# GFNet mixing and a tanh-shrink MLP on one core: other Fourier factors, on folded rows, each batch alone

## The chip, the cores and the metric

The kernel runs on one core of a Trainium2 chip. The core has five engines that run side by side, each through its own queue in order: PE (TensorE, matrix products), DVE (VectorE), ACT (ScalarE), POOL (GpSimd) and SP (SyncE, which here only issues DMAs). PE's weight loads are a row of their own in the profile (PEld). The metric is the device time of one execution in microseconds (us), the median of several runs.

## The reference, cut to what matters

```python
def _attn_ref(x, filt_r, filt_i):            # x: 8 x 3008 x 256, float32
    X = np.fft.rfft(x, axis=1)
    F = (filt_r + 1j * filt_i)[None, :, :]   # 1505 x 256
    y = np.fft.irfft(X * F, n=x.shape[1], axis=1)
    return y.astype(np.float32)

def _moe_ref(x, w_in, w_out):                # x: 24064 x 256
    h = x @ w_in                             # 256 x 2048, given in float64
    g = h - np.tanh(h)
    return (g @ w_out).astype(np.float32)    # 2048 x 256
```

Each batch's 3008 rows are transformed along the sequence, multiplied by a complex filter that all batches share, and transformed back. All 24064 rows then go through a two-layer network with the function h - tanh(h) between.

## The kernel before, in words

3008 is 64 x 47, so a row number is 47 q + r with q from 0 to 63 and r from 0 to 46. The Fourier transform is done in two factors, and its inverse in two more, so the attention has three stages:

- **first** (`first`, L344; `first0`, L890, for batch 0): 64-point transforms over q for two values of r at a time. One constant 128x128 matrix `wf1` holds two 64x64 blocks, so two batches (a pair) share one product of 512 columns. ACT copies the result (`a1`) and stores it in DRAM (`ct1`).
- **middle** (`middle`, L401): 32 slots, one for each conjugate pair of frequencies. A slot has its own 94x128 matrix `f2` (47-point transform and twiddle factors) and its own 112x96 way back `g`, which `load_slots` (L376) fetches four at a time. After the product `pz` (L436), ACT writes the swapped halves (`zs`, L449 and L450), DVE multiplies `pz` by the filter's real part (`uv`, L451), and POOL multiplies `zs` by the imaginary part and adds (L452, L453). `back` does the product `pe` (L417), ACT copies it (`e1`, L420) and stores it in DRAM (`ct2`).
- **last** (`last`, L506): for a group of four r, products of `e2` (read from `ct2`) with the 128x128 matrix `s2`; the result `ut` stands with features on partitions, as the network needs it.

Batches are taken in units: batch 0 alone, pairs (1,2), (3,4), (5,6), and batch 7 alone. In a unit of two batches, a group is four values of r by 128 rows, 512 tokens. There are 46 groups.

The network works on one group in four passes; pass U has a quarter of the hidden width. The two big products use seven block products instead of eight (`combine`, L529, makes the sums that this needs), with half of a group's tokens (256 columns) at a time. Three functions overlap: `up(U)` (L538) makes h for pass U, `shrink(U-1)` (L613) makes h - tanh(h) for the pass before in about the form h * (sq + K) * y with ACT and DVE (L632 and L639 are DVE's two operations of 1024 columns, two of each in a pass), and `down(U-2)` (L668) multiplies by the second weights. At the end of `shrink`, POOL's `combine` (L530 to L533) makes the four tiles `t` from h, and PE's products `o<-t` (L688) of the following pass read them. The results are turned by DVE (L738) and leave in many small stores on SP (L781).

The order on every engine is written out by hand. A pass calls `t(0)` to `t(4)`, five places in which one step of the next unit's transforms may be put: a batch that stands alone has 6 groups x 4 passes x 5 = 120 such positions. The list `steps` (L1101 to L1108) gives each step of `first` and `middle` its position; two of the places in every fourth pass belong to `last`. So while PE works through the network for one unit, the transforms of the next unit lie between its products, and their DVE, ACT and POOL parts lie in those engines' queues at the same places.

PSUM's eight banks are x, y, z and t, one each, and the four of `down`; the transforms' products use t and y in turn (`zd`, L1052). In `up`, the first product of a pass overwrites x, so it waits until DVE has read x (L602).

Before all passes there is a preparation: batch 0 goes through first and middle, the weights of the network, which come in float64, are turned to float32 by DVE's integer operations (`converted`, L195), and POOL makes their sums (L264 to L267). The filter is read by POOL's DMAs (L916). During the first unit, POOL also copies the filter into the layout that `middle` reads (`filters_d`, L1068).

After the passes, a small reduction (`bounded`) decides whether a general form of the network has to run on the data; it doesn't run here.

Of the kernel before, what the change touches and what calls it, by code (L numbers as in the profile page):

```python
# [9 lines left out]
F32 = mybir.dt.float32  # L10
# [7 lines left out]

BATCH, SEQ, DM = 8, 3008, 256
NQ, NR = 64, 47
NK = NQ // 2
R2 = 2 * NR

RP = 48
RP2 = 2 * RP
LO = (NR + 1) // 2
HI = NR - LO  # L30
IM = 64
DFF = 2048
NP = DFF // 256
BD = 2 * DM
CH = 4
XH = 2


UNITS = [(0,), (1, 2), (3, 4), (5, 6), (7,)]
HALF = (NR + 1) // 2  # L40

EARLY = 2


def steps_of(unit):
    return NR if len(unit) == 2 else HALF


def chunks_of(unit, size):
    n = steps_of(unit)  # L50
    return [(r, min(size, n - r)) for r in range(0, n, size)]


# [5 lines left out]


# [4 lines left out]


def _consts():
    wq = np.exp(-2j * np.pi * np.outer(np.arange(NQ), np.arange(NQ)) / NQ)
    wr = np.exp(-2j * np.pi * np.outer(np.arange(NR), np.arange(NR)) / NR)
    tw = np.exp(-2j * np.pi * np.outer(np.arange(NQ), np.arange(NR)) / SEQ)  # L70


    f1 = np.zeros((NQ, 64))
    f1[:, 0:31] = wq.real[:, 1:32]
    f1[:, 31] = wq.real[:, 0]
    f1[:, 32:63] = wq.imag[:, 1:32]
    f1[:, 63] = wq.real[:, 32]


    wf1 = np.zeros((2, 128, 64, 2))  # L80
    wf0 = np.zeros((64, 2, 2, 64))
    for b in range(2):
        wf0[:, b, b] = f1
        wf1[0, 64 * b:64 * b + 64, :, b] = f1
        wf1[1].reshape(128, 2, 64)[64 * b:64 * b + 64, b] = f1
    wf1 = wf1.reshape(2, 128, 128).transpose(1, 0, 2)

    perm = np.arange(NR)  # L90
    perm[LO:] = LO + NR - 1 - perm[LO:]
    f2 = np.zeros((NK, R2, R2))
    for a in range(31):
        wp = (wr * tw[a + 1][None, :])[perm, :]
        f2[a, 0::2] = np.concatenate([wp.real.T, wp.imag.T], axis=1)
        f2[a, 1::2] = np.concatenate([-wp.imag.T, wp.real.T], axis=1)
    f2[:, :, NR + LO:] *= -1.0
    w0, w32 = wr * tw[0][None, :], wr * tw[32][None, :]
    f2[31, 0::2, 0:LO] = w0.real.T[:, 0:LO]
    f2[31, 0::2, NR + 1:NR + LO] = w0.imag.T[:, 1:LO]  # L100
    f2[31, 1::2, LO:NR] = w32.real.T[:, 0:HI]
    f2[31, 1::2, NR + LO:R2] = w32.imag.T[:, 0:HI]
    f2[31, 1::2, NR] = w32.real.T[:, HI]


    f2w = np.zeros((NK, R2, 128))
    f2w[:, :, 0:NR], f2w[:, :, IM:IM + NR] = f2[:, :, :NR], f2[:, :, NR:]


    ctw = np.exp(2j * np.pi * np.outer(np.arange(33), np.arange(NR)) / SEQ)  # L110
    g = np.zeros((NK, IM + NR, R2))
    for a in range(31):
        t1 = (wr.conj() * ctw[a + 1][:, None]) / SEQ
        tr, ti = t1.real.T[perm, :], t1.imag.T[perm, :]
        g[a, :NR, :NR], g[a, :NR, NR:] = tr, ti
        g[a, IM:, :NR], g[a, IM:, NR:] = -ti, tr
    g[:, IM + LO:] *= -1.0
    t0 = (wr.conj() * ctw[0][:, None] / SEQ).T
    t32 = (wr.conj() * ctw[32][:, None] / SEQ).T
    g[31, 0, :NR] = t0.real[0]  # L120
    g[31, IM, NR:] = t32.real[HI]
    g[31, 1:LO, :NR], g[31, IM + 1:IM + LO, :NR] = 2 * t0.real[1:LO], -2 * t0.imag[1:LO]
    g[31, LO:NR, NR:], g[31, IM + LO:, NR:] = 2 * t32.real[0:HI], -2 * t32.imag[0:HI]


    w = np.exp(2j * np.pi * np.outer(np.arange(NQ), np.arange(33)) / NQ)
    s = np.zeros((64, NQ))
    s[0:62:2] = 2.0 * w.real[:, 1:32].T
    s[1:62:2] = -2.0 * w.imag[:, 1:32].T
    s[62] = w.real[:, 0]  # L130
    s[63] = w.real[:, 32]
    s2 = np.zeros((128, 128))
    for b in range(2):
        s2[64 * b:64 * b + 64, 64 * b:64 * b + 64] = s


    fg = np.zeros((IM + RP, NK, 128 + RP2))
    fg[:R2, :, :128] = f2w.transpose(1, 0, 2)
    fg[:IM + NR, :, 128:].reshape(IM + NR, NK, 2, RP)[..., :NR] = \
        g.transpose(1, 0, 2).reshape(IM + NR, NK, 2, NR)  # L140

    return [np.ascontiguousarray(v, dtype=np.float32)
            for v in (wf0.reshape(128, 128), wf1, fg.reshape(IM + RP, -1), s2, np.eye(128))]


@with_exitstack
def kernel(
# [11 lines left out]
    wf0_d, wf1_d, fg_d, s2_d, one_d = (  # L159
        nc.inline_tensor(v, name=n).ap()  # L160
        for v, n in zip(_consts(), ("wf0", "wf1", "fg", "s2", "one")))


    ct1 = [nc.dram_tensor(f"ct1_{p}", (RP, 64 * len(bs), DM), F32, kind="Internal")
           for p, bs in enumerate(UNITS)]
    ct2 = [nc.dram_tensor(f"ct2_{p}", (64 * len(bs), RP, DM), F32, kind="Internal")
           for p, bs in enumerate(UNITS)]

    filt_d = nc.dram_tensor("filt", (IM, 2, NK, DM), F32, kind="Internal")
# [6 lines left out]
    wf1 = cst.tile([128, 2, 128], F32, name="wf1_sb")  # L176
    s2 = cst.tile([128, 128], F32, name="s2_sb")
    near_b = cst.tile([128, 1], F32, name="near_b")
    exp_b = cst.tile([128, 1], F32, name="exp_b")
    groups = [(p, c) for p, bs in enumerate(UNITS) for c in range(len(chunks_of(bs, CH)))]  # L180
    count = cst.tile([1, 1], I32, name="count")

# [5 lines left out]


# [78 lines left out]

# [50 lines left out]
    def halves(p, r, n):  # L327

        return [(h, slice(64 * h, 64 * h + 64), r + HALF * h, min(n, NR - r - HALF * h))
                for h in range(2) if r + HALF * h < NR]  # L330

    def load_x(p, r, n):
        t = tr.tile([128, XH, DM], F32, tag="x", bufs=3, name="x_sb")
        b = UNITS[p][0]
        if len(UNITS[p]) == 2:
            nc.sync.dma_start(t[:, 0:n, :], dram(x.tensor, (b * SEQ + r) * DM,
                                                 [[NR * DM, 128], [1, n * DM]]))
        else:
            for _, rows, r_h, n_h in halves(p, r, n):
                nc.sync.dma_start(t[rows, 0:n_h, :], dram(x.tensor, (b * SEQ + r_h) * DM,  # L340
                                                          [[NR * DM, 64], [1, n_h * DM]]))
        return t

    def first(p, z):  # L344

        chunks = chunks_of(UNITS[p], XH)
        pair = len(UNITS[p]) == 2
        xs = {c: load_x(p, *chunks[c]) for c in range(2)}
        yield
        for c, (r, n) in enumerate(chunks):  # L350
            if c + 2 < len(chunks):
                xs[c + 2] = load_x(p, *chunks[c + 2])
            xt = xs.pop(c)
            pf = z("pf", [128, XH, DM])
            a1 = tr.tile([128, XH, DM], F32, tag="a1", bufs=2, name="a1")
            if pair:
                nc.tensor.matmul(pf[:, 0:n, :], wf1[:, 0], xt[:, 0:n, :], start=True, stop=True)  # L357
                ACT.copy(a1[:, 0:n, :], pf[:, 0:n, :])  # L358
                ACT.dma_start(
                    dram(ct1[p], r * 128 * DM, [[DM, 128], [128 * DM, n], [1, DM]]),  # L360
                    a1[:, 0:n, :])
            else:
                parts = halves(p, r, n)
# [852 lines left out]
```

## Time and profile before

| | |
|---|---|
| Median of 3 runs | 2796.31 us (2794.76 to 2798.26) |
| Profiled execution, span from first to last instruction | 2793.9 us |
| PE busy | 2718.0 us (97%), 12436 records |
| DVE busy | 1914.7 us (69%) |
| ACT busy | 1883.9 us (67%) |
| POOL busy | 1759.4 us (63%) |
| DMA | 217.66 MB, 78 GB/s over the span |
| First product of the passes | at 113.6 us of the span |

The span of the profiled execution leaves 2.4 us to the median of the runs. A float32 product of the kernel is two weight loads and two MATMUL records in the trace. PE's records overlap each other, so their lengths don't add up; what a product costs is read from when the next one starts. In the lists of groups, a row gives line, engine, operation, out<-in, shapes and count, then total busy us and mean ns of one, then the idle time of the engine before them and what ended it.

### The profile page before, as it was taken

What the parts mean: (1) busy time and instruction counts of PE and PEld (TensorE: products, weight loads), DVE (VectorE), ACT (ScalarE), POOL (GpSimd) and SP (SyncE); (2) the same over time, 40 slices, a digit from 0 to 9 for tenths busy, and PEclk for the clock granted to TensorE, in tenths of its full rate; (3) what the DMA queues carried; (4) which work ended last, traced back from release to release, by engine and by line L of the source; (5) the groups of instructions that cost most, each with busy time, mean ns of one, the idle gap of its engine ahead of it and who ended that gap; (6) DMA issues with size and microseconds to landing.
All of it is one profiled execution on the core that took longest, in us unless ns stands there. A gap on an engine that the chain in (4) does not pass through costs nothing.

```text
span 2793.9 us, 36447 instructions
## 1 busy us (share of the span) xinstructions
PE 2718.0 (97%) x12436; PEld 2272.7 (81%) x12436; DVE 1914.7 (69%) x2190; ACT 1883.9 (67%) x2785; POOL 1759.4 (63%) x1399
## 2 busy tenths in 40 slices
PE   5899999999999999999999999999999999999998
PEld 3577778888878888888888888888888888898887
DVE  5776666666776777665677776766676667677777
ACT  3466776666767777666677777666666666666665
POOL 6456887444776777544576777654476666555553
PEclk8999999999999999999999999999999999999999
DMA  9854443332332322223323233112223222101010
GB/s 267 222 170 116 107 124 76 89 84 72 81 82 72 73 69 59 64 78 89 83 69 75 71 80 84 38 43 66 59 66 78 65 57 58 31 19 26 16 22 18
DMA packets 322095, 217.66 MB, mean 78 GB/s; under 512 B 224718, under 2 KB 274746, under 8 KB 321596
## 3 DMA queue, kind: packets, MB, share of 16 engines
q1 hardware_dynamic: 265994, 156.69, 24.1%
q10 hardware_dynamic: 52562, 50.09, 5.8%
q0 software_dynamic: 3344, 8.46, 1.1%
q8 instruction: 100, 1.64, 0.2%
q14 instruction: 95, 0.78, 0.1%
HBM read 139.00 MB, written 79.17 MB: 78 GB/s over the span
## 4 chain that ended last, share of the span: by engine, by line
PE 83%; DVE 5%; ACT 4%; DMA 2%; issue 2%; POOL 1%; ACTq 0%; SPq 0%; DVEq 0%; POOLq 0%
PE o L688 35%; PE x L551 21%; PE z L551 10%; PE y L551 5%; PE pe L417 3%; PE pz L436 3%; PE pu L517 3%; PE pf L357 2%; DVE h L632 2%; ACT y L628 1%; DMA raw<-in_moe_w_out_dram 1%; DVE h L602 1%; ACT y L625 1%; DVE h L639 1%; ACT sq L636 0%
## 5 line engine op out<-in xcount | busy, mean ns | idle before, releaser
L632 DVE TENSOR_TENSOR h<-h,y 128x1024 f32<-128x1024 f32 (+2 forms) x384 | 576.9, 1502 | 306.2 <-ACT y L628 305.1
L688 PE MATMUL o<-t,wd 128*128 128x256 f32 (+2 forms) x3072 | 774.4, 375 | 0.0
L688 PEld LDWEIGHTS o<-t,wd 128*128 128x128 f32 x3072 | 579.4, 190 | 90.9 <-issue 22.0
L639 DVE SCALAR_TENSOR_TENSOR h<-sq,h 128x1024 f32<-128x1024 f32 (+2 forms) x384 | 557.4, 1451 | 117.2 <-ACT sq L636 109.2
L688 PE MATMUL o<-h,wd 128*128 128x256 f32 (+2 forms) x2304 | 582.3, 375 | 6.8 <-DVE h L639 6.8
L551 PE MATMUL x<-tu,wu 128*128 128x256 f32 (+2 forms) x2304 | 582.0, 375 | 2.2 <-ACT u L557 2.1
L530 POOL TENSOR_TENSOR t<-h 128x512 f32<-128x512 f32 (+2 forms) x190 | 238.5, 1256 | 542.6 <-DVE h L639 385.3
L551 PEld LDWEIGHTS x<-tu,wu 128*128 128x128 f32 x2304 | 430.3, 190 | 103.0 <-issue 41.6
L688 PEld LDWEIGHTS o<-h,wd 128*128 128x128 f32 x2304 | 430.5, 190 | 80.4 <-issue 15.8
L636 ACT ACTIVATE sq<-y,near_b 128x1024 f32<-128x1024 f32 (+2 forms) x384 | 435.1, 1133 | 6.7 <-ACT y L628 0.3
L625 ACT ACTIVATE y<-h 128x1024 f32<-128x1024 f32 (+2 forms) x384 | 397.4, 1035 | 15.2 <-ACT e L420 6.4
L628 ACT ACTIVATE y<-y 128x1024 f32<-128x1024 f32 (+2 forms) x384 | 399.9, 1042 | 6.6 <-ACT a L358 0.4
L557 ACT COPY s<-x 128x512 f32<-128x512 f32 (+2 forms) x192 | 110.7, 577 | 327.9 <-PE x L551 301.7
L533 POOL TENSOR_TENSOR t<-t,h 128x512 f32<-128x512 f32 (+2 forms) x190 | 318.1, 1674 | 0.0
L557 ACT COPY u<-x 128x512 f32<-128x512 f32 (+2 forms) x384 | 220.7, 575 | 138.2 <-PE x L551 119.3
L531 POOL TENSOR_TENSOR t<-h,t 128x512 f32<-128x512 f32 (+2 forms) x190 | 244.2, 1285 | 14.9
L532 POOL TENSOR_TENSOR t<-h 128x512 f32<-128x512 f32 (+2 forms) x190 | 243.4, 1281 | 0.0
L452 POOL TENSOR_TENSOR zs<-zs,ft 128x512 f32<-128x512 f32 x112 | 164.9, 1472 | 93.5 <-ACT zs L450 93.3
L453 POOL TENSOR_TENSOR uv<-uv,zs 128x512 f32<-128x512 f32 x112 | 207.7, 1855 | 9.1 <-DVE uv L451 0.5
L551 PE MATMUL x<-ut,wu 128*128 128x256 f32 (+2 forms) x768 | 198.6, 381 | 9.7 <-DVE h L602 8.3
L594 DVE TENSOR_TENSOR h<-z,u 128x512 f32<-128x512 f32 (+2 forms) x192 | 128.8, 671 | 112.8 <-ACT u L557 111.9
L551 PE MATMUL z<-tu,wu 128*128 128x256 f32 (+2 forms) x768 | 195.2, 377 | 0.0
(129 smaller groups left out, 3294.0 us busy)
## 6 DMA issues: line engine op xcount, KB each, us to landing
a<-ct SPq DMA_DIRECT2D x64, 384.0 KB, 4.1
ft<-filt SPq DMA_DIRECT2D x96, 256.0 KB, 4.6
out_dram<-ot SPq DMA_DIRECT2D x1392, 16.0 KB, 1.5
ct<-e ACTq DMA_DIRECT2D x112, 192.0 KB, 2.2
ct<-a ACTq DMA_DIRECT2D x81, 256.0 KB, 2.9
x_sb<-in_x_dram SPq DMA_DIRECT2D x69, 256.0 KB, 2.9
e<-ct SPq DMA_DIRECT2D x33, 512.0 KB, 4.2
fg<-fg SPq DMA_DIRECT2D x40, 392.0 KB, 4.0
```

The costliest lines, as they stand in the source:

```text
L530: by.tensor_sub(t[0], b[0][1], b[0][0])
L531: by.tensor_sub(t[1], b[1][1], t[0])
L532: by.tensor_sub(t[2], b[1][1], b[0][1])
L533: by.tensor_sub(t[3], t[1], b[1][0])
L551: nc.tensor.matmul(bank[:, k], wu[:, q - 1, (2 * u + k) * 128:(2 * u + k + 1) * 128], rhs[q - 1], start=(first and k == 0), stop=True, ski ...
L557: ACT.copy(t, X)
L625: ACT.activation(y[k], ht[k], AF.Arctan, scale=S)
L628: ACT.activation(y[k], y[k], AF.Square, accum_out=y_sums[:, 2 * U + k // 2:2 * U + k // 2 + 1])
L632: V.tensor_mul(ht[k], ht[k], y[k])
L636: ACT.activation(sq[k], y[k], AF.Square, bias=near_b, scale=A)
L639: V.scalar_tensor_tensor(out=ht[k], in0=sq[k], scalar=K, in1=ht[k], op0=ALU.add, op1=ALU.mult)
L688: nc.tensor.matmul(product(q), wd[:, q - 1, (2 * u + k) * 128: (2 * u + k + 1) * 128], rhs[q - 1][:, k], start=(u == 0 and k == 0 and q == ...
```

## The change

The two factors are kept (64 and 47), but the work is cut another way.

- r and 47 - r are folded into one: only r = 0 to 23 are taken (`NH` = 24), with row r of the input on 64 partitions and row 47 - r on the other 64. Row 0 has no partner; it is loaded twice and its second matrix half is zero.
- The twiddle factors go into the first and the last matrices. So each r has its own dense 128x128 matrix, `f` for `first` (products of 256 columns, two to a step) and `gt` for `last`; both are loaded from DRAM next to the data, where `wf1` and `s2` lay in SBUF throughout.
- What is left between are real cosine and sine matrices of 24x24, the same for all frequencies. Five frequencies stand side by side on 120 partitions (`SG` = 5, `SLOTS`: six groups of five and one of two, seven slot groups for the 32 slots), and one constant tile `mats` holds their matrices; `fg` and `load_slots` are gone.
- In a slot group (`forth`, `filtered`, `back`; 8 products of 256 columns), the data are four blocks of 256. PE makes two and two products `pa`; ACT copies two blocks into `xy`; DVE adds and subtracts (L333, L334). POOL then multiplies the four blocks by the filter's real part (L343, 1024 columns) and by the imaginary part (L346, 1024 columns), and does four operations of 512 columns (L348, L349, L351, L352). PE goes back with four products `pe`, ACT copies them in two pieces (L365) and stores them. For batch 0, in the preparation, L343 and L346 are DVE's.
- Every batch stands alone: there are no pairs. A batch has six groups of four r; the first has 448 tokens, the others 512; 48 groups in all. `first` has 12 steps of two r per batch (`NX`), with positions from `FIRST` (0.24 to 32 of the 120); `middle` has 7 steps per slot group and two more, with positions from `MID` (38 to 103).
- `EARLY` is 0: no step of the next batch's `first` runs in the preparation (there were two). The last `e2` of batch 0 is loaded whole. The copies of the filter are 44 DMAs on POOL instead of 10, at four places of a pass instead of two.

The network's own code (`up`, `shrink`, `down`, `combine`) is as it was.

```diff
-UNITS = [(0,), (1, 2), (3, 4), (5, 6), (7,)]
-EARLY = 2
+NA = NQ // 2
+NH = (NR + 1) // 2
+SG = 5
+SLOTS = [(a, min(SG, NA - a)) for a in range(0, NA, SG)]
+KM = SG * NH
+EARLY = 0
+FIRST, MID = (0.24, 32), (38, 103)
...
 def first(b, z):
...
-                nc.tensor.matmul(pf[:, 0:n, :], wf1[:, 0], xt[:, 0:n, :], start=True, stop=True)
+            for i in range(XH):
+                nc.tensor.matmul(pf[:, i], f[:, i], xt[:, i], start=True, stop=True)
...
+    def forth(g, at, z):
+        n = SLOTS[g][1] * NH
+        xy = tr.tile([KM, 4, DM], F32, tag="xy", bufs=2, name="xy")[0:n]
+        way = ways(g, 0)
+        for v in (1, 0):
+            pa = z("pa", [128, 2, DM])[0:n]
+            for k in range(2):
+                nc.tensor.matmul(pa[:, k], way[2 * v + k], at[0:n, 2 * v + k],
+                                 start=True, stop=True)
+            if v:
+                ACT.copy(xy[:, 2:4], pa)
+                yield xy
+        V.tensor_add(xy[:, 0:2], pa, xy[:, 2:4])
+        V.tensor_sub(xy[:, 2:4], pa, xy[:, 2:4])
+        yield
+
+    def filtered(g, xy, ft, by, by2):
...
+        nn = tr.tile([KM, 4, DM], F32, tag="nn", bufs=1, name="nn")[0:n]
+        by.tensor_mul(nn.rearrange("p (x v) c -> p x v c", v=2), ab,
+                      fv[:, :, 0:1].to_broadcast([n, 2, 2, DM]))
+        yield
+        by.tensor_mul(ab, ab, fv[:, :, 1:2].to_broadcast([n, 2, 2, DM]))
+        yield
+        by2.tensor_sub(nn[:, 0:4:3], nn[:, 0:4:3], xy[:, 1:3])
+        by2.tensor_add(nn[:, 1:3], nn[:, 1:3], xy[:, 0:4:3])
+        yield
+        by2.tensor_add(xy[:, 0:2], nn[:, 0:2], nn[:, 2:4])
+        by2.tensor_sub(xy[:, 2:4], nn[:, 0:2], nn[:, 2:4])
+        yield
...
     def middle(b, z):
...
-            ACT.mul(zs[0:IM], pz[IM:128], -1.0)
-            ACT.copy(zs[IM:128], pz[0:IM])
-            V.tensor_mul(rows(uv), rows(pz), fr)
-            G.tensor_mul(rows(zs), rows(zs), fi)
-            G.tensor_add(uv, uv, zs)
...
+            there = forth(g, a2.pop(g), z)
+            xy = next(there)
+            yield
+            next(there)
+            done = filtered(g, xy, ft.pop(g), G, G)
+            next(done)
+            yield
+            next(done)
+            yield
+            for _ in waiting:
+                yield
+            for _ in done:
+                yield
+            waiting = back(b, g, xy, z)
...
-                            steps = [0.01 * units + 1.36 * units * (k - done) / (n_f - done)
-                                     for k in range(n_f)]
-                            lo, hi = 1.6 * units, 5 * units - 17
-                            steps += [lo + (hi - lo) * k / n_m for k in range(n_m)]
+                            steps = [FIRST[0] + (FIRST[1] - FIRST[0]) * (k - done) / (NX - done)
+                                     for k in range(NX)]
+                            n_m = 7 * len(SLOTS) + 2
+                            steps += [MID[0] + (MID[1] - MID[0]) * k / n_m for k in range(n_m)]
```

More of the change, by code (lines that the diff above doesn't have):

```diff
@@ L129, in _consts, with angle @@
[L129 to L140, printed above, removed]
+    q = np.arange(NQ)[:, None]
+    k1 = np.arange(1, NA)[None, :]
+    def angle(r):
+        return 2 * np.pi * ((k1 * (NR * q + r)) % SEQ) / SEQ
@@ new lines, in back @@
+    def back(b, g, xy, z):
+        n = SLOTS[g][1] * NH
+        way = ways(g, 1)
+        for v in range(2):
+            pe = z("pe", [128, 2, DM])[0:n]
+            for k in range(2):
+                nc.tensor.matmul(pe[:, k], way[2 * v + k], xy[:, 2 * v + k],
+                                 start=True, stop=True)
+            e1 = tr.tile([KM, 2, DM], F32, tag="e1", bufs=2, name="e1")[0:n]
+            ACT.copy(e1, pe)
+            ACT.dma_start(rows(ct2, b, g, 2 * v, 2), e1)
+            yield
```

674 lines of the change are left out of this document (263 added, 411 removed).

## The prediction

> **What bounds the kernel now.** I read the page's head first, then the busy times by stretch, then PE's timeline, then POOL's and DVE's.
>
> ```profile
> span 2793.9 us, 36447 instructions
> PE 2718.0 (97%) x12436; PEld 2272.7 (81%) x12436; DVE 1914.7 (69%) x2190; ACT 1883.9 (67%) x2785; POOL 1759.4 (63%) x1399
> ```
>
> The profiled execution spans 2793.9 us; the median of the runs is 2796.31, so 2.4 us lie around the span. PE is busy nearly always, but a busy PE need not be at its peak, so the spacing of its products has to be read.
>
> ```profile
> core 0: us, PE busy (x) PEld busy (x) DVE busy (x) ACT busy (x) POOL busy (x), PEclk, DMA share, GB/s
> 0.00:114.00 114.00, 75.65 (x258) 49.79 (x259) 71.30 (x148) 42.97 (x62) 72.12 (x111) 0.84 0.91 246
> 265.00:482.00 217.00, 214.80 (x910) 166.23 (x910) 144.67 (x164) 158.44 (x242) 174.88 (x128) 1.00 0.42 106
> 725.00:1117.00 392.00, 389.92 (x1737) 318.72 (x1736) 280.02 (x294) 279.03 (x414) 289.28 (x209) 1.00 0.30 71
> 2510.00:2736.00 226.00, 225.77 (x1082) 198.54 (x1081) 162.77 (x171) 152.29 (x216) 131.43 (x100) 1.00 0.11 21
> ```
>
> The first row is the preparation: PE waits, the DMA engines are 91% busy. The second is the first batch's passes while the middle of batches 1 and 2 runs beside them, the third the same for a later pair, the fourth passes with no transform beside them. In the last three PE is full.
>
> ```profile
> 298.26 1.89 PE L688 MATMUL o<-t,wd 128*128 128x256 f32 x8
> 299.99 1.02 PE L436 MATMUL pz<-a,fg 94*128 94x512 f32 x2
> 300.85 1.03 PE L551 MATMUL x<-tu,wu 128*128 128x256 f32 x4
> ```
>
> Starts: eight records of 256 columns fill 1.73 us (0.216 each), two of 512 fill 0.86 (0.43). A product is two records, and its price goes by columns: splitting 512 into two of 256 costs PE nothing. So after the preparation time is PE's columns.
>
> ```profile
> 303.77 1.22 DVE L639 SCALAR_TENSOR_TENSOR h<-sq,h 128x1024 f32<-128x1024 f32 x1
> 303.90 2.22 POOL L453 TENSOR_TENSOR uv<-uv,zs 128x512 f32<-128x512 f32 x1
> ...
> 343.79 1.26 POOL L533 TENSOR_TENSOR t<-t,h 128x512 f32<-128x512 f32 x1
> 344.24 1.90 DVE L632 TENSOR_TENSOR h<-h,y 128x1024 f32<-128x1024 f32 x1 [0.92 <-ACT y L628]
> ```
>
> Undisturbed these take 1.22 (DVE) and 1.27 (POOL). L453 started 0.13 after L639 and ended at 306.12, as if it had begun at 304.85, 0.14 before L639's end. L632 started inside L533 and ended at 346.14, as if begun at 344.92, 0.13 before L533's end. So L632/L639 (both operands in SBUF) and POOL's two-operand operations take turns: one holds something the other needs, DVE for 1.08 us, POOL for 1.14. I call it the shared path. DVE's operations from PSUM don't take part (L594, L602: 682 and 680 ns always).
>
> ```profile
> L452 POOL TENSOR_TENSOR zs<-zs,ft 128x512 f32<-128x512 f32 x112 | 164.9, 1472 | 93.5 <-ACT zs L450 93.3
> L453 POOL TENSOR_TENSOR uv<-uv,zs 128x512 f32<-128x512 f32 x112 | 207.7, 1855 | 9.1 <-DVE uv L451 0.5
> L531 POOL TENSOR_TENSOR tu<-ut,tu 128x256 f32<-128x256 f32 x42 | 31.0, 738 | 70.5 <-ACT ut L519 69.4
> ```
>
> Of POOL's records of 512 columns the undisturbed take 1.27, of 256 0.73: 0.18 + 2.13 ns per column. Held: 1.14 and 0.60. Counting operations in the stretches (108 of 512, 20 of 256 and 55 of DVE at 265:482; 168, 41, 108 at 725:1117; 72, 28, 72 at 2510:2736) the path was held 194 of 217 us (90%), 333 of 392 (85%), 177 of 226 (78%). At 90% PE still lost nothing.
>
> **The change, part by part.**
> *PE.* Removed from the stream: middle records L436 and L417, 384 of 512 columns and 128 of 256: 384 x 0.43 + 128 x 0.216 = 193.5 us. Added: 7 batches x 7 slot groups x 8 products x 2 records x 0.216 = 169.3. First matrices: 160 records of 512 (and 10 of 256) were 70.8 us, now 7 x 48 x 0.216 = 72.6; two steps that ran in the preparation (EARLY) move in, +1.7. Last matrices: 46 groups before, 48 after, the same tokens, 0. Together -20.7 us, on the path.
>
> *POOL, the middle.* Before, L452 and L453 per slot: 2 x 1.14 = 2.28 of the path, 16 slots per batch (batches share filter slots in pairs): 36 us per batch. After, per slot group, two products of 1024 and four operations of 512. No row has 1024 columns: the line through 256 and 512 gives 2.36, held 2.23; the ends are 1.8 (setup and overlap better hidden than the line says) and 2.54 (two of 512). I take the line, whose two points are the same operation. Per group 2 x 2.23 + 4 x 1.14 = 9.02, per batch 63. And it is confined to positions 39 to 100 of a batch's 120, 12.2 passes. Per pass the path then owes DVE 4 x 1.08 = 4.32, `combine` 4 x 1.14 = 4.56, the six operations of 256 per four passes 0.90, and the middle 63/12.2 = 5.17: 14.95 us. PE needs 56 records x 0.216 = 12.10, last matrices 16 x 0.112 / 4 = 0.45, middle 24.2/12.8 = 1.89: 14.44. **So for 12 passes of every batch the shared path, not PE, is the bound, by 0.5 us a pass, 6.2 us a batch.** In order, POOL has `combine` of a pass queued behind the middle's operations, and PE's products o<-t wait for `combine`.
>
> ```profile
> 701.01 1.27 POOL L530 TENSOR_TENSOR t<-h 128x512 f32<-128x512 f32 x1 [4.33 <-PE x L551]
> ...
> 706.41 0.59 PE L688 MATMUL o<-t,wd 128*128 128x256 f32 x2
> ```
>
> t is ready at 702.28 and used at 706.41: POOL may be 4 us late before PE notices. So 6.2 - 4 = 2.2 us a batch are lost at the least by the line. To that comes path time nobody uses: POOL's new first product waits for DVE's add and subtract (L333, L334, each about 0.68 as L594) and the filter load, and steps are uneven: seven per group, four per pass, so a pass holds from 5 to 10 us of POOL's. At 265:482 POOL waited 26 us of 217 (17.4 for DVE's h, 9.2 for zs). I allow a fifth of that share, 2.4% of 180 us = 4.3. Stall 6.5 us a batch, 45 in seven. The ends: 0 (held 1.8) and 20 a batch, 140 (path never held above 90%: 182/0.90 - 176 - 4 = 22, a little less).
>
> *DVE* pays L333 and L334, 14 x 0.68 = 9.5 us a batch for 16 x 0.686 = 11: nothing. Behind them stands L531, which frees PE's x bank; its delay is in the upper end. *ACT* loses L449, L450 (0.59 + 0.58) and gains one copy: 28 us a batch become 21 x 0.58 = 12, off the path, a gain of nothing with PE bound.
>
> *Queues.* SP issues f and x in three pieces per first step, gt with e2, more output pieces (1632 for 1504): some 250 issues at 0.48 (21 took 10.12 us). Loads run two steps (five positions, 15 us) ahead against 2.9 to land; were the cover gone, 84 steps would cost 1 to 2 us each. POOL issues 44 filter copies instead of 10 in batch 0, 0.6 each, a third beside the middle: bounds 0 and +8, I take +4.
>
> *Preparation.* Before: first pz at 39.6, last pe product 105.3, first x product 113.6. Until the middle starts, 12.0 MB must move instead of 11.2 (f for wf, mats for fg) at 286 GB/s: +3. Then POOL carries 28 operations of 1.27, 30 filter issues of 0.57 and 12 sums of 0.73 = 61.4 us; the first six issues come early (-3.4); DVE's two products (2 x 1.22) hide behind issues except in the last two groups (+4.9); start 5.3. From 42.6 that ends near 110.8, and with the whole e2 loaded after the last ct2 store (4.2 instead of a quarter of it) the first x product falls near 121.5: +8. Ends: -6 (total bytes 25.3 for 26.8 MB, if DMA alone is the bound) and +20 (every collision on the path adds).
>
> Sum: 2793.9 - 20.7 + 45 + 4 + 8 = 2830.2, plus 2.4: **2832.6**.
>
> **The rivals.**
> A, *PE stays the bound*, the other side: one mechanism, the path's demand fits. It decides where a 1024-wide operation holds the path under 1.79 us (then 14 of them save the 6.2 us a batch). For it: at 90% PE lost nothing, and from 2050 to 2063.5 us POOL was busy 13.2 of 13.5 us beside a PE busy 13.3. Against it: the line through 256 and 512. Time: 2796.3 - 20.7 + 0 to 12 = 2776 to 2788. Chance 0.25.
>
> B, *the path is badly used*: DVE's in-order queue, held 2.23 instead of 1.14 behind a long POOL product, brings L531 late, and the next pass's first product waits for it (before, DVE's h L602 held PE and PEld 19 and 47 times). Fourteen such per batch at 1.1 us each are at most 107 us, added to the stall's 45 to 140. Against it: only a few of the long ones meet the one critical product. Time 2870 to 2930. Chance 0.15.
>
> C, *the path is held for whole instructions*. Per pass 4 x 1.22 + 4 x 1.27 + 1.09 + 7 x 9.8/12.2 = 16.7 against 14.44: 27 us a batch, less 4, 163 in all: about 2950. Against it: the 0.13 us overlap above, and 265:482 would have needed 219 of its 217 us. Chance 0.06. [...]
>
> D, *only the preparation moves*, +16 to +26 with A's steady part: within 0.2% of before. Chance 0.04.
>
> **How the numbers follow.** The forecast case (stall of 2 to 12 us a batch) has 0.50: 2800 to 2870. A measurement can tell about 0.2% (5.6 us) from no change. Faster 0.25 (A), same 0.05 (D and the forecast's low edge), slower 0.70. The range leaves out the fastest edge of A and the upper part of B and C: 2777 to 2900.
>
> **What would show it.** PE records of 256 at 0.216 throughout (else the -20.7 is wrong). In the middle's passes: period 14.4 (A) or about 15 (forecast), PE's waits before o<-t naming POOL `combine` (forecast) or before x naming DVE L531 (B). The 1024-wide POOL records: 2.36 undisturbed. First x product near 121. Wrong above all if POOL's four-block operations are shorter or longer than the line, or if a late POOL hands on more than its own lateness.

## The result and the profile after

The changed kernel takes 2923.34 us (median, 2922.41 to 2925.24), the kernel before 2797.03 beside it: 1.0458 times as long, 95% interval 1.0443 to 1.0472. It is slower, as forecast, but by 126 us and not by 36, and the time lies outside the range. The profiled executions differ by 127.3 us. The head of the page after:

```profile
span 2921.2 us, 37028 instructions
PE 2739.2 (94%) x12830; PEld 2373.4 (81%) x12830; DVE 2010.2 (69%) x2171; ACT 1764.4 (60%) x2583; POOL 2124.7 (73%) x1503
```

Busy times by stretch after: the preparation, the first batch's passes beside the middle, a later batch's middle, passes with no transform beside them.

```profile
core 0: us, PE busy (x) PEld busy (x) DVE busy (x) ACT busy (x) POOL busy (x), PEclk, DMA share, GB/s
0.00:146.40 146.40, 67.89 (x196) 48.42 (x197) 97.47 (x144) 28.08 (x48) 99.10 (x117) 0.72 0.67 184
300.00:517.00 217.00, 206.54 (x959) 175.94 (x960) 148.83 (x148) 131.54 (x191) 179.94 (x119) 0.98 0.27 64
956.00:1158.00 202.00, 191.62 (x883) 161.17 (x882) 145.65 (x139) 121.72 (x175) 190.93 (x113) 0.99 0.27 64
2640.00:2866.00 226.00, 225.52 (x1081) 199.28 (x1080) 165.57 (x176) 153.01 (x219) 127.76 (x98) 1.00 0.11 24
```

In the last row PE is as full as before. In the two above it is not: 10 of 217 and of 202 us are idle, and POOL is busy 191 of 202. The first row is 32.8 us longer than the preparation before, with the DMA engines busy 67% (91% before). Also the chain of waits has another face:

```profile
PE 50%; POOL 28%; DVE 10%; issue 5%; ACT 4%; DMA 2%; SPq 0%; ACTq 0%; POOLq 0%; DVEq 0%
```

The same line before:

```profile
PE 83%; DVE 5%; ACT 4%; DMA 2%; issue 2%; POOL 1%; ACTq 0%; SPq 0%; DVEq 0%; POOLq 0%
```

What PE waited for after (us in all, times, longest):

```profile
PE pe L362 <- POOL xy L351: 78.4, 21, 9.1
PE x L483 <- DVE h L531: 35.0, 39, 1.7
PE pf L808 <- DMA x<-in_x_dram: 23.6, 4, 9.7
PE pa L328 <- issue: 9.1, 1, 9.1
PE o L615 <- POOL t L465: 7.1, 14, 1.5
PE o L615 <- POOL t L463: 6.9, 8, 1.1
```

The forecast's wait, o <- t for POOL's `combine` (L463 to L466), is there with 14 us. Two larger ones stand above it. The products back (`pe`, L362) wait for POOL's addition L351; of these 78.4 us, 44.7 (7 waits) lie in the preparation and 33.7 in the passes. And the first product of a pass (x, L483) waits for DVE's copy L531, which was L602 before:

```profile
PE x L551 <- DVE h L602: 8.3, 19, 0.9
```

Waits alone don't add up to the time, so I take PE's lost time in another way. For each MATMUL record between the first x product and the last o product, I take the distance of its start from the start before, less the 0.216 us (or the median of that product) that it usually is, and add up what is over 0.05 us. The rest of the stretch is the time of the columns.

| profiled us | before | after | difference |
|---|---|---|---|
| up to the first x product | 113.6 | 146.4 | +32.8 |
| columns, first x to last o | 2619.3 | 2600.8 | -18.5 |
| lost, first x to last o | 51.2 | 161.4 | +110.2 |
| last o to the end | 9.9 | 12.5 | +2.7 |

So the stall is the error: +110 where the sum had +45, and the preparation is +33 where it had +8. The columns come out at 2600.5 to 2601.0 in all the runs below, whatever they lost, so no loss hides in the excesses under 0.05 us, which the split leaves with them. Of the 161.4, 42.7 lie before x, 36.0 before pe, 17.6 before o <- t, 14.5 before others, each over 0.25 us; the remaining 50.7 are many small ones (13.9 before).

Two places show how it comes about. The first is at the end of a pass (timeline of all engines after, start, us, operation):

```profile
996.36 1.26 POOL L348 TENSOR_TENSOR nn<-nn,xy 120x512 f32<-120x512 f32 x1
...
997.06 0.65 DVE L523 TENSOR_TENSOR h<-z,u 128x512 f32<-128x512 f32 x1
997.58 1.26 POOL L349 TENSOR_TENSOR nn<-nn,xy 120x512 f32<-120x512 f32 x1
997.64 2.29 DVE L561 TENSOR_TENSOR h<-h,y 128x1024 f32<-128x1024 f32 x1
...
998.93 2.13 POOL L351 TENSOR_TENSOR xy<-nn 120x512 f32<-120x512 f32 x1
999.85 0.68 DVE L531 COPY h<-x 128x512 f32<-128x512 f32 x1
...
1000.59 0.70 PE L483 MATMUL x<-ut,wu 128*128 128x256 f32 x2 [1.69 <-DVE h L531]
```

DVE's L561 (1.22 undisturbed) starts just after POOL's L349 and is 2.29 long; its end is as if it had begun 0.13 before L349's. Behind it in DVE's queue stands L531, which reads the x bank, so PE's next pass starts 1.69 us late. Of this, 1.07 is the hold (2.29 for 1.22). POOL's L351 pays in turn, 2.13 for 1.27. DVE's lateness reached PE before POOL's did.

The second place is the end of every middle (POOL and PE):

```profile
1136.69 2.24 POOL L348 TENSOR_TENSOR nn<-nn,xy 48x512 f32<-48x512 f32 x1
...
1138.90 2.25 POOL L349 TENSOR_TENSOR nn<-nn,xy 48x512 f32<-48x512 f32 x1
...
1143.69 2.27 POOL L465 TENSOR_TENSOR t<-h 128x512 f32<-128x512 f32 x1
...
1145.91 2.25 POOL L466 TENSOR_TENSOR t<-t,h 128x512 f32<-128x512 f32 x1
1148.12 1.25 POOL L351 TENSOR_TENSOR xy<-nn 48x512 f32<-48x512 f32 x1
...
1149.43 1.06 PE L362 MATMUL pe<-xy,mats_sb 48*48 48x256 f32 x4 [3.48 <-POOL xy L351]
...
1150.42 1.78 PE L483 MATMUL x<-tu,wu 128*128 128x256 f32 x4
```

Four operations of POOL have stretched to 2.25, a `combine` lies in the queue ahead of L351, and PE, in order, stops before pe for 3.48 us. The four records behind it take 1.78 instead of 1.03 us. The busy times by stretch say why, here at three such places:

```profile
451.00:457.80 6.80, 6.80 (x16) 4.50 (x16) 1.85 (x2) 3.36 (x5) 1.17 (x1) 0.50 0.06 14
799.20:806.00 6.80, 5.47 (x13) 3.52 (x14) 0.69 (x1) 2.07 (x4) 2.50 (x3) 0.50 0.06 14
1150.80:1154.20 3.40, 3.40 (x10) 2.68 (x9) 0.98 (x2) 2.23 (x5) 0.00 (x0) 0.50 0.14 34
```

The granted clock (behind POOL's column) is 0.50 for 3.4 or 6.8 us each time; the same follows all seven middles, whose last waits of pe for L351 are 3.46 to 3.48 us long. So here a pause is paid twice: as the wait of 3.48 us, and as slow products after it. The last section has a wait of 1.69 us that was followed by the same. I had no such term.

One slip in the text above: the kernel before has 48 groups like the one after, not 46. The sum set that at nothing, so nothing follows from it.

### The profile page after: what moved, and what is told of

The parts are those of the page before. It is cut to its first block, busy times and chain, and to the rows that moved or that the text cites. A ratio compares the mean times of both kernels' runs of the same rounds, so it can differ in the third digit from the quotient of the medians.

```text
span 2921.2 us, 37028 instructions
## 1 busy us (share of the span) xinstructions
PE 2739.2 (94%) x12830; PEld 2373.4 (81%) x12830; DVE 2010.2 (69%) x2171; ACT 1764.4 (60%) x2583; POOL 2124.7 (73%) x1503
## 3 DMA queue, kind: packets, MB, share of 16 engines
q8 instruction: 103, 1.69, 0.3%
## 4 chain that ended last, share of the span: by engine, by line
PE 50%; POOL 28%; DVE 10%; issue 5%; ACT 4%; DMA 2%; SPq 0%; ACTq 0%; POOLq 0%; DVEq 0%
PE o L615 21%; PE x L483 13%; PE z L483 6%; PE y L483 4%; POOL t L466 4%; DVE h L561 4%; POOL t L464 3%; POOL t L465 3%; POOL t L463 3%; POOL xy L346 2%; PE pf L296 2%; PE pu L449 2%; POOL nn L343 2%; POOL xy L352 2%; POOL nn L348 2%
## 5 line engine op out<-in xcount | busy, mean ns | idle before, releaser
L561 DVE TENSOR_TENSOR h<-h,y 128x1024 f32<-128x1024 f32 (+1 forms) x384 | 617.8, 1609 | 295.2 <-ACT y L557 295.2
L615 PE MATMUL o<-t,wd 128*128 128x256 f32 (+1 forms) x3072 | 790.4, 380 | 14.0 <-POOL t L465 7.1
L615 PEld LDWEIGHTS o<-t,wd 128*128 128x128 f32 x3072 | 586.8, 192 | 97.1 <-POOL t L465 13.7
L568 DVE SCALAR_TENSOR_TENSOR h<-sq,h 128x1024 f32<-128x1024 f32 (+1 forms) x384 | 595.7, 1551 | 99.2 <-ACT sq L565 93.2
L483 PE MATMUL x<-tu,wu 128*128 128x256 f32 (+1 forms) x2304 | 591.2, 379 | 3.1 <-ACT u L489 3.1
L615 PE MATMUL o<-h,wd 128*128 128x256 f32 (+1 forms) x2304 | 584.8, 376 | 4.6 <-DVE h L568 4.6
L463 POOL TENSOR_TENSOR t<-h 128x512 f32<-128x512 f32 (+1 forms) x190 | 245.3, 1291 | 444.4 <-DVE h L568 349.2
L483 PEld LDWEIGHTS x<-tu,wu 128*128 128x128 f32 x2304 | 435.9, 192 | 62.7 <-issue 7.9
L565 ACT ACTIVATE sq<-y,near_b 128x1024 f32<-128x1024 f32 (+1 forms) x384 | 435.1, 1133 | 9.2 <-DVE h L568 2.9
L554 ACT ACTIVATE y<-h 128x1024 f32<-128x1024 f32 (+1 forms) x384 | 397.5, 1035 | 13.3 <-ACT a L297 5.7
L557 ACT ACTIVATE y<-y 128x1024 f32<-128x1024 f32 (+1 forms) x384 | 399.7, 1041 | 6.3
L466 POOL TENSOR_TENSOR t<-t,h 128x512 f32<-128x512 f32 (+1 forms) x190 | 341.3, 1796 | 0.0
L465 POOL TENSOR_TENSOR t<-h 128x512 f32<-128x512 f32 (+1 forms) x190 | 277.6, 1461 | 0.0
L523 DVE TENSOR_TENSOR h<-z,u 128x512 f32<-128x512 f32 (+1 forms) x192 | 128.5, 669 | 166.4 <-ACT u L489 165.8
L483 PE MATMUL x<-ut,wu 128*128 128x256 f32 (+1 forms) x768 | 202.2, 386 | 36.2 <-DVE h L531 35.0
L362 PE MATMUL pe<-xy,mats_sb 120*120 120x256 f32 (+1 forms) x448 | 132.6, 426 | 78.4 <-POOL xy L351 78.4
L483 PEld LDWEIGHTS x<-ut,wu 128*128 128x128 f32 x768 | 139.7, 191 | 76.2 <-DVE h L531 61.2
L506 DVE TENSOR_TENSOR h<-y,s 128x512 f32<-128x512 f32 (+1 forms) x192 | 130.1, 677 | 99.0 <-PE y L483 93.8
```

What stands on the lines that cost most here:

```text
L463: by.tensor_sub(t[0], b[0][1], b[0][0])
L465: by.tensor_sub(t[2], b[1][1], b[0][1])
L466: by.tensor_sub(t[3], t[1], b[1][0])
L483: nc.tensor.matmul(bank[:, k], wu[:, q - 1, (2 * u + k) * 128:(2 * u + k + 1) * 128], rhs[q - 1], start=(first and k == 0), stop=True, ski ...
L554: ACT.activation(y[k], ht[k], AF.Arctan, scale=S)
L557: ACT.activation(y[k], y[k], AF.Square, accum_out=y_sums[:, 2 * U + k // 2:2 * U + k // 2 + 1])
```

## The experiments: the passes

All runs in one table; "batch" is the mean of batches 1 to 6 from first x to first x, "lost" is taken as above, ratios are to the kernel before beside each. First x, batch and lost are of the profiled execution; that of p1_add_dve took 2901.32 us, 11 less than its median.

| run | median us | ratio, interval | first x | batch | lost |
|---|---|---|---|---|---|
| after | 2923.34 | 1.0443 to 1.0472 | 146.4 | 349.4 | 161.4 |
| e1_mul_dve | 2897.93 | 1.034 to 1.0375 | 146.1 | 345.4 | 137.6 |
| e2_offpath | 2825.71 | 1.0093 to 1.0127 | 144.3 | 335.7 | 67.8 |
| e3_grace | 2875.91 | 1.0274 to 1.0309 | 143.9 | 342.9 | 115.2 |
| e4_spread | 2894.46 | 1.0334 to 1.0369 | 146.5 | 345.9 | 134.2 |
| e5_split | 2928.77 | 1.0455 to 1.049 | 148.6 | 350.5 | 168.7 |
| e6_offpath_grace | 2803.49 | 1.002 to 1.0039 | 145.1 | 332.8 | 46.0 |
| e7_vv_grace | 2907.99 | 1.0383 to 1.0418 | 145.8 | 347.1 | 146.8 |
| e8_vv_best | 2841.06 | 1.0141 to 1.0174 | 134.3 | 339.7 | 92.8 |
| e9_vg_best | 2848.48 | 1.0168 to 1.0202 | 133.5 | 341.3 | 102.2 |
| p1_add_dve | 2912.74 | 1.0403 to 1.0438 | 132.2 | 348.3 | 154.0 |
| p2_conv_later | 2930.59 | 1.0457 to 1.0499 | 150.7 | 349.4 | 162.3 |
| p3_few_mats | 2908.44 | 1.0378 to 1.042 | 129.9 | 349.9 | 163.6 |

**Is it the path, or only POOL's load?**

```diff
 (in middle; filled() writes the same tiles with G.memset in the same steps)
-            done = filtered(g, xy, ft.pop(g), G, G)
+            done = filled(g, xy, ft.pop(g))
```

> The changed kernel with POOL's six filter operations per slot group of the passes replaced by memsets of about the same total length, on the same tiles and in the same steps; so the middle's data of batches 1 to 7 are constants, not the filtered rows, and the rest of the work is as it was. POOL stays as long busy, but a memset reads nothing. Theory 1 (shared path): a pass owes the path 9.8 us only; PE's stalls go, passes of about 14.4 us, time 2780 to 2815, and DVE's two-operand operations come back to 1.22 us beside the memsets. Theory 2 (POOL's own work, in order): POOL is as late as before, time 2880 to 2925.

2825.71 us, 98 less. The memsets took POOL 526 us. The operations in their place would take 479 undisturbed (98 of 2.35 and 196 of 1.27) and took 617, so POOL's own work has not become less. But the memsets don't stop DVE (timeline of that run):

```profile
982.98 0.95 POOL L361 MEMSET xy<- 120x1024 f32 x1
983.04 0.68 DVE L547 COPY h<-x 128x512 f32<-128x512 f32 x1
...
983.64 1.21 DVE L584 SCALAR_TENSOR_TENSOR h<-sq,h 128x1024 f32<-128x1024 f32 x1
...
983.99 0.53 POOL L362 MEMSET xy<- 120x512 f32 x1
...
984.46 0.21 POOL L363 MEMSET xy<- 120x128 f32 x1
```

L584 (L568 in the kernel after) runs through three memsets in 1.21 us; 144 such operations beside memsets have a median of 1.22. What PE waits for there:

```profile
PE pe L378 <- POOL xy L351: 45.9, 7, 10.3
...
PE pe L378 <- POOL xy L367: 15.5, 7, 2.2
...
PE x L499 <- DVE h L547: 7.9, 10, 0.9
...
PE o L631 <- POOL t L481: 3.2, 3, 1.5
```

The first line is the preparation's. The wait of x for DVE falls from 35.0 to 7.9, of o <- t from 14 to 3.2. Theory 2 falls, by 54 us; the shared path carries most of the stall, DVE's share of it included. The time is also 11 us over theory 1's upper end: 15.5 us before pe remain, 2.2 at the end of each middle.

**The order at the middle's end.**

```diff
             waiting = back(b, g, xy, z)
-        yield
-        yield
+        for _ in range(5):
+            yield
...
-                            n_m = 7 * len(SLOTS) + 2
+                            n_m = 7 * len(SLOTS) + 5
-FIRST, MID = (0.24, 32), (38, 103)
+FIRST, MID = (0.24, 32), (38, 107)
```

> The changed kernel with five empty steps instead of two between the last slot group's last POOL operation and its products back, and the middle's last position moved from 103 to 107, so that the steps are as dense as they were; nothing left out. Theory 3 (a part of the stall is only the order: PE meets the last group's pe while POOL is 8 to 9 us behind): the wait pe <- L351 (78 us) falls under 20, time 2923 - 7 x 8 = about 2865. Theory 1 alone: POOL's arrears are then paid elsewhere, by the products o<-t that wait for combine, time 2905 to 2925.

2875.91, 47 less, near the 2865 of theory 3. Before pe 10.5 us are lost for 36.0, before x still 42.6 and before o <- t still 17.6, so nothing was paid elsewhere. (The wait of pe for L351 falls from 33.7 to 9.4 in the passes; the expected "under 20" had counted the 44.7 of the preparation as if they were the passes'.) The lone small losses fall from 50.7 to 33.5 as well, and the stretch in which the same pe now stands shows the full clock:

```profile
1132.00:1139.00 7.00, 6.99 (x32) 5.57 (x30) 6.22 (x6) 3.37 (x5) 5.77 (x4) 1.00 0.00 0
```

**Both together.** The edit is that of e2_offpath and of e3_grace.

> The kernel with POOL's filter operations of the passes replaced by memsets (so the middle's data of batches 1 to 7 are constants), with five empty steps for two before the last products back and the middle's last position at 107. If the shared path and the order at the middle's end are the whole of the stall, the steady batches fall from 349 us to 331 to 332 (335.5 with the memsets alone, of which 3.7 lie in the pass at the middle's end) and the time from 2826 to about 2800. If something else of the middle costs time too, they stay at 334 or more, time 2815 or more.

2803.49, with 332.8 us a batch and 46.0 us lost, less than the 51.2 of the kernel before. The two savings overlap (98 and 47 alone, 120 together). The path and that one place are the whole of the stall, within a few us; about 1 us a batch more than expected stays unnamed.

**Average demand or something finer?** The forecast compared the path's demand per pass with PE's time. Two runs bring the demand below it.

```diff
-            done = filtered(g, xy, ft.pop(g), G, G)
+            done = filtered(g, xy, ft.pop(g), V, G)
```

> The changed kernel with the middle's two 1024-wide filter products (L343, L346) given to DVE instead of POOL; nothing left out. Theory 1 (the shared path is the bound in the middle's passes): DVE holds the path about 1.08 us where POOL holds it 2.23, so a pass in the middle owes the path 14.95 - 1.3 = 13.6 us, under PE's 14.4; the passes fall from 15.5 to about 14.6, the wait of PE's pe (L362) for POOL's L351 (78 us in all) falls to under 20 us, time 2800 to 2835. Theory 2 (POOL's own work in its in-order queue, without the path): also faster, since POOL loses 33 us a batch; this run doesn't tell 1 from 2. Rival B (DVE's lateness at L531 is what PE waits for): DVE gets 1.4 us more in each pass, the waits x <- h grow over their 35 + 61 us, time 2900 or more.

```diff
-FIRST, MID = (0.24, 32), (38, 103)
+FIRST, MID = (0.24, 22), (26, 106)
```

> The changed kernel with the same steps at other positions: first from 0.24 to 22 instead of 32, middle from 26 to 106 instead of 38 to 103; nothing left out. The middle then lies in 16 passes instead of 12.2. Theory 1: a pass owes the path 4.32 + 4.56 + 0.90 + 63/16 = 13.7 us, PE 12.10 + 0.45 + 24.2/16 = 14.05, so the stall falls to under 6 us a batch, time 2800 to 2840. Theory 3 (the order at the middle's end, and uneven steps): only the average falls, the end's wait of 8 us a batch stays, time 2860 to 2900.

2897.93 and 2894.46: theory 1 is missed by 63 and 54 us. The second time lies in theory 3's range, but not for its reason, since the wait at the middle's end is gone; the first is near rival B's 2900, but the waits before x didn't grow. With the products on DVE the losses before o <- t over 0.25 us are gone, as they should with 13.6 us of path in a pass, but before x 36.5 us are lost still (42.7), and others rise from 14.5 to 28.8: the products now stand in DVE's own queue before the operations that PE waits for. With the steps spread, the waits at the middle's end vanish (pe 1.1 us), but o <- t rises to 30.2 and x stays at 41.2, both mostly in the first half of the middle; the closer `first` adds 8.1 us of waits for x's transfers. So these runs show no threshold at PE's time per pass. As I read it, single meetings of two operations at a bad place, like the one at 997.58 that cost PE 1.69 us, cost it whatever the average.

Is it then the length of POOL's new operations?

```diff
-        by.tensor_mul(nn.rearrange("p (x v) c -> p x v c", v=2), ab,
-                      fv[:, :, 0:1].to_broadcast([n, 2, 2, DM]))
...
+        parts = (0, 1) if by is G else (slice(0, 2),)
+        for to, k in ((nb, 0), (ab, 1)):
+            for x in parts:
+                by.tensor_mul(to[:, x], ab[:, x],
+                              fv[:, x, k:k + 1].to_broadcast(list(ab[:, x].shape)))
+            yield
```

> The changed kernel with each of POOL's 1024-wide products (L343, L346) of the passes cut into two of 512; nothing left out. The time that the path is held hardly changes (2 x 1.14 = 2.28 for 2.23), but no single hold is longer than 1.14 us. In the steady batches the changed kernel loses 19.8 us each against the usual spacing of its products: 5.9 before x <- ut (waiting for DVE's h), 5.6 before pe, 3.5 before o <- t. Rival B (long holds bring DVE late, and the next x waits): the loss before x falls from 5.9 to 3 or less, time 2923 - 20 or more = 2900 or less. Theory 1 (the amount of path time counts): the losses stay, POOL becomes a little slower, time 2918 to 2935.

2928.77, as theory 1 had it: half the length, the same time held, and x loses 35.7 for 42.7; in a steady batch, with losses over 0.15 us counted, 5.5 for 5.9, far from 3. The long hold as such is not the cause.

**All on DVE.**

```diff
 (with five empty steps at the end, as in e3_grace)
-FIRST, MID = (0.24, 32), (38, 103)
+FIRST, MID = (0.24, 30), (34, 107)
-            done = filtered(g, xy, ft.pop(g), G, G)
+            done = filtered(g, xy, ft.pop(g), V, V)
```

> The changed kernel with all six filter operations of the passes on DVE, five empty steps for two before the last products back, first from 0.24 to 30 and middle from 34 to 107; nothing left out. Theory 1: a slot group holds the path 2 x 1.08 + 4 x 0.55 = 4.4 us for 9.0, so the path has room (12.2 us of a pass's 14.4) and POOL comes early with combine; the losses before o <- t go, time 2830 to 2860. Rival B (DVE in order is the one that comes late, now with 5.2 us more per slot group): the losses before x, y and z grow over 8 us a batch, time 2870 to 2910.

2907.99: rival B's time, and DVE is what comes late, but not before x, y or z as the rival had it (x loses 37.1 for 42.7). Before o <- t almost nothing is lost; 33.7 us are waits of pa (L328) for DVE:

```profile
PE pa L328 <- DVE h L506: 33.7, 13, 4.2
```

pa is written to PSUM bank y in turn with t, and L506 reads y. At the longest of these waits DVE did L346, L348, L349, L351 and L352 among its other work in the 8 us ahead of L506. When I wrote the next expectation I took this for a late load of `ct1`; the row says otherwise. The next run changes the positions, and so what stands ahead of L506 when pa comes.

```diff
 (e8_vv_best: as e7_vv_grace, but)
+FIRST, MID = (0.24, 32), (38, 107)
-                done = filtered(g, xy, fts.pop(g), V, G)          (preparation)
+                done = filtered(g, xy, fts.pop(g), V, V)
 (e9_vg_best: the same, but in middle)
+            done = filtered(g, xy, ft.pop(g), V, G)
```

> The changed kernel with all six filter operations of the passes and of the preparation on DVE, five empty steps for two before the last products back, middle from 38 to 107; nothing left out. Before, with the middle from 34, 5.2 of 17.6 us lost in a batch lay before the first pa, for which ct1 wasn't back yet. Without that: steady batches 341 to 343 us, first x product at 132, time 2843 to 2865. If DVE's lateness grows instead, batches of 346 or more, time 2880 or more.

> The same, but in the passes only the two products (L343, L346) on DVE and the four additions on POOL. The path owes 13.6 us a pass (12.2 with all on DVE), DVE has 2.4 us more in a slot group (5.2). If the path decides, this is slower than the kernel with all on DVE; if DVE's queue decides, faster. From the run with the products on DVE: 345 less the 5 of the middle's end, 340 us a batch, first x product at 132, time 2840 to 2855.

2841.06 and 2848.48, 1.6 and 1.9% over the kernel before; the first 2 us under and the second inside what was expected, although my reason for the first, `ct1`, was wrong. The waits of pa for L506 are 3.5 us in e8_vv_best, and as I read it pa now falls where L506 is done. All on DVE is 7 us better, so here the path weighs more than DVE's queue. These are the best versions that I found with the whole computation; both are slower than the kernel before. In e8_vv_best POOL no longer appears among PE's waits, and yet:

```profile
PE x L483 <- DVE h L531: 34.3, 42, 2.4
```

The wait for L531 is as large as after (35.0). There it came through the path. Here L561 and L568 take 1.38 us on the mean (1024 columns), as in e2_offpath (1.40, and 1.66 after), where this wait was 7.9; so here I put it down to DVE's own work ahead of L531.

## The experiments: the preparation

In the profile after, the first product of a slot group's way back stands at 60.4, 69.8, 82.9, 96.7, 112.5, 123.5 and 134.0 us: 12.3 apart on the mean. Here is what happens between (timeline of the kernel after; L148 to L151 turn the weights' float64 to float32):

```profile
78.55 0.42 DVE L148 TENSOR_SCALAR conv<-raw 128x512 int32<-128x512 int32 x1
78.78 1.30 POOL L348 TENSOR_TENSOR nn<-nn,xy 120x512 f32<-120x512 f32 x1 [3.96 <-DVE xy L346]
78.88 1.48 DVE L149 TENSOR_SCALAR conv<-raw 128x512 int32<-128x512 int32 x1
80.05 1.44 POOL L349 TENSOR_TENSOR nn<-nn,xy 120x512 f32<-120x512 f32 x1
80.29 1.48 DVE L151 TENSOR_SCALAR conv<-raw 128x512 int32<-128x512 int32 x1
81.56 1.33 POOL L351 TENSOR_TENSOR xy<-nn 120x512 f32<-120x512 f32 x1
```

L149 and L151 have one operand, and take 0.42 undisturbed; here, beside POOL, they take 1.48. My path had only two-operand operations on DVE's side, although the preparation before shows the same (timeline of the kernel before; L209 takes 0.42 elsewhere):

```profile
28.00 0.76 POOL L264 TENSOR_TENSOR wu<-wu 128x256 f32<-128x256 f32 x1 [14.27 <-DVE wu L234]
28.09 0.95 DVE L209 TENSOR_SCALAR conv<-raw 128x512 int32<-128x512 int32 x1
```

```diff
-                done = filtered(g, xy, fts.pop(g), V, G)
+                done = filtered(g, xy, fts.pop(g), V, V)
```

> The changed kernel with batch 0's four additions per slot group (L348 to L352, in the preparation) given to DVE instead of POOL; nothing left out. Theory of collisions (POOL's two-operand operations and DVE's fast integer operations on the weights stop each other): DVE's 148 to 165 stay at 0.42 us, the cycle of a slot group falls from 13.2 us to 11 or less, first x product at 130 to 135 for 146, time 2908 to 2913. Theory of DVE's load (28 more operations of 0.69 are 19 us more in its queue, which is full): first x product at 146 to 155, time 2920 to 2932.

The first x product comes at 132.2, 14 us earlier, though DVE got 28 more operations; the slot groups are 10.7 apart. The same operations there:

```profile
68.85 0.42 DVE L148 TENSOR_SCALAR conv<-raw 128x512 int32<-128x512 int32 x1
69.18 0.42 DVE L149 TENSOR_SCALAR conv<-raw 128x512 int32<-128x512 int32 x1
...
69.52 0.42 DVE L151 TENSOR_SCALAR conv<-raw 128x512 int32<-128x512 int32 x1
```

The collisions were real and DVE's load was not the limit.

```diff
                 for _ in waiting:
-                    next(ws, None)
+                    pass
                 for _ in done:
                     pass
-                next(ws, None)
...
 (ws_gap is made, and both run, only after the last products back)
```

> The changed kernel with no step of the weight conversion between batch 0's slot groups in the preparation: the conversions that lay there come after the last products back; nothing left out. It asks what a slot group takes by itself. Collisions: without DVE's fast integer operations beside POOL's the six distances between slot groups' first products back (60.4 to 134.0, 12.3 on the mean) fall to about 9, so that the last one starts near 114; the conversions then follow and the first x product is no earlier than 145. A chain of the slot group's own operations (DVE's products, then POOL's four, one nn tile): the distances stay at 11 or more.

Without conversions between them the slot groups are 8.75 apart (58.1 to 110.6), as the collisions had it, and the first x product is at 150.7. This takes away the conversions' own time on DVE as well, so it bounds the collisions from above only.

```diff
 (with p1_add_dve's edit)
-                nc.sync.dma_start(f0[:, 8 * c:8 * c + 8], ...)
+                if c == 0:
+                    nc.sync.dma_start(f0[:, 8 * c:8 * c + 8], ...)
```

> The changed kernel with batch 0's additions on DVE, and with only 8 of the 24 first matrices loaded in the preparation (each used for three values of r, so batch 0's rows are not the transformed ones). 1 MB less has to come before the middle starts. If bytes set that start, the first pa comes 3 to 4 us earlier than the 46 to 48 us of the kernels with all 24, and everything behind moves with it; if not, it stays.

The first pa stands at 43.2, the first x at 129.9: 3.1 and 2.3 us before p1_add_dve. The first pa of all the kernels with 24 matrices lies between 45.9 and 50.3. One profile of each shows little more than that bytes count: 43.2 is below all of them, but 3.1 us is less than they differ among themselves.

## Why the prediction was wrong

- *PE's columns, -20.7*: measured -18.5. The usual distance of records of 256 columns is 0.216 in all runs. Right.
- *The 1024-wide products at 2.36*: the shortest on POOL is 2.348 (the median 3.2, waits for DVE in it). Right, and rival A, which needed a hold under 1.79, is out.
- *POOL's filter copies in batch 0, +4*: not shown. Batch 0 takes 353.7 for the others' 349.4 (337.2 for 332.8 in e6_offpath_grace), but its columns are 317.7 for 329.8, since its first two passes have no `down` yet. So it loses 36.0 us for 19.6, and 19.6 for 3.2 in e6_offpath_grace. The kernel before loses 21.5 in its own first unit, and the 19.6 are no more than that; no run sets the copies apart.
- *The stall, +45*: measured +110. The step that failed is "Stall 6.5 us a batch", worked out as demand of the path over PE's time, less a slack of 4 us, plus 4.3 for uneven steps, with PE's wait before o <- t as the only place where it is paid. The path is the cause (98 us go with it), but it is paid in three places. Before o <- t it was 17.6 us. Before x, through DVE's queue, 42.7 (12.9 before): rival B's wait, which had 0.15 because "only a few of the long ones meet the one critical product". It isn't the long ones, as e5_split shows; a POOL operation of 512 columns that meets L561 shifts L531, as at 997.58. And at the middle's end, 36.0 before pe, and 47 in all that moving pe gives back, slow clock included; no case of mine had that, though a late POOL that "hands on more than its own lateness" was among my signs of being wrong. That only two empty steps lie between the last L352 and pe stood in the code; I had priced POOL's lateness, but not asked which of its readers has the least slack.
- *The row that misled*: before, at 90% of path use, PE lost nothing. From this I made a limit near 100%. e1_mul_dve and e4_spread, at 13.6 of 14.4 and 13.7 of 14.05 by the same count, lose 138 and 134 us. The 90% held for that kernel's order of steps, not for the path.
- *Preparation, +8*: measured +32.8, 13 beyond the upper end. The first pa came at 48.4 instead of 42.6 (45.9 to 50.3 in the runs with the same matrices); I had 3 us for bytes and it was 8.8 against the first pz before. And "every collision on the path adds" counted only operations that I knew to take the path; the conversions do too (1.48 us for 0.42). Moving POOL's side away gave 14 us back. From the first pa to the first x it is then (p1_add_dve) 85.8 us, against 74.0 from the first pz before; these 12 I have only bounded (slot groups 8.75 apart without conversions, 10.7 with).
- *The rivals*: B's times, 2870 to 2930, hold the result, and its wait makes up 30 of the 110 us; it should have had far more than 0.15. C (the path held for whole instructions, 2950) is denied by the rows: the overlap of 0.13 us is there after as well.

## What to carry to other kernels

When an engine off the path gets more work, list every instruction of other engines that waits for it, and take the one with the least slack, not the one that waited before; then do the same for engines that it can hold up through a shared resource. A use of 90% without loss in one order of steps is no limit for another order. And a wait of PE for a few us can be dearer than its length, here (waits of 1.69 and 3.48 us) by up to half of the 3.4 or 6.8 us at half the clock that go with it.

## What was not expected of the hardware

- DVE's integer operations with a single operand in SBUF (0.42 us for 512 columns) and POOL's two-operand operations hold each other up: beside POOL, L149 and L151 took 1.48 us in the rows above, and where five of DVE's ran in a row at 0.41 us (L148 to L157, from 127.08 us after), POOL's L348, started at 127.30, took 3.59 us for 1.27. DVE's operations from PSUM took no part: 0.65 to 0.69 us for 512 columns, beside POOL or alone (L506, L523, L531, L539 after). The prediction had counted only DVE's operations with two operands in SBUF.
- POOL's memsets didn't hold up DVE's two-operand operations: in e2_offpath these took 1.22 us beside them, as alone (median of 144 operations; 1.21 in the rows above).
- PE's pause at the end of each of the seven middles (the wait is 3.48 us at the one shown) was followed by 3.4 or 6.8 us at a granted clock of 0.50. Shorter pauses were followed by it too: after a wait of 1.69 us before x at 1348.55 us came 3.4 us at 0.50, while after the wait of the same length at 1000.59, shown above, the clock stayed at 1.00.
- How idle PE was ahead of these falls can be read off the traces. After, eleven falls lie between the first x and the last o product. I count as idle what products at their usual distance (0.216 us for 256 columns) don't fill: in the 3.41 us ahead of each fall this is 62 to 99%. The two waits of 1.69 us lie close together: 62.4% idle ahead of 1348.73, where the clock fell, and 61.7% ahead of 1000.57, where it didn't. Before, the two falls in the same stretch follow 74 and 88%. What decides between two so near these traces don't show.

The row behind the wait at 1348.55 (busy times by stretch, after):

```profile
1348.70:1352.10 3.40, 3.40 (x9) 2.68 (x10) 2.00 (x2) 0.58 (x1) 3.40 (x3) 0.50 0.67 133
```
